# Widening a four-column constants tile to 128 columns in a fused retention and two-layer kernel

## The chip, the cores and the metric

The kernel runs on one core of one Trainium2 chip. The metric is the device time of one execution in microseconds; the kernel before takes 929.96 us, the median of three runs that lie between 928.1 and 932.1 us.

## The reference

The reference is a retention stage (attention with a decaying mask and no softmax) over 4 batches, 8 heads, 576 positions and head size 64, whose output is read as x with 2304 tokens and 512 features. Two layers follow, both 512 to 2048 to 512:

```
ret = (scale * q @ k.T) * Dmat            # Dmat[i, j] = gamma_h ** (i - j) for j <= i, else 0
x = (ret @ v), heads side by side         # 2304 x 512
h = x @ w_in;  g = max(0.01 * h, h);  x = g @ w_out       # layer 1
h = x @ w2_in; g = h - tanh(h);       out = g @ w2_out    # layer 2
```

## The kernel before, in words

**Precision.** Every matmul of the two layers works on a pair of fp32r tiles: a number is held as a rounded high part and the remainder (`xh` and `xl`; index 0 and 1 of `wp` and of `g`). A product is three matmuls: high by high, high by low, low by high. On the tensor engine each matmul has a stationary operand of 128 by 128, which a weight load brings in, and a moving operand of 128 by 512 or 128 by 256.

**Steps.** A layer goes over four groups of four blocks of 128 hidden features, and in each group over blocks of 512 tokens and one of 256. One step is one block of tokens with one block of features. Layer 1 has 60 steps of 512 tokens and 12 of 256 behind the retention stage, which itself carries the first 12 steps (256 tokens each) between its own matmuls. Layer 2 has 64 steps of 512 and 16 of 256. For each step the order of emission is the order on the engines:

- `h_mm` (L181): 12 matmuls, x moving (`xh`, `xl`, `xh` for each of four slices of features), the weights `wp` stationary.
- `act_a` and `chain`: ScalarE, VectorE and GpSimd make g from h. In layer 1 this is L193, L215, L224, L225; in layer 2 it is L201 to L207, L218 to L222, L224, L225. GpSimd has two operations for each step of layer 2: the product v (L203) and the low part of g (L225).
- `o_mm` (L251), two steps later: in layer 1 g moves and `wp` is stationary, in layer 2 `wp` moves and g is stationary. 12 matmuls in a step of 512 tokens.
- `evac` adds the result to `acc` at each fourth step.

While a group runs, the weights of the next are loaded as 64-bit numbers into `st`, narrowed on VectorE into `cw` and split into `wp` (L161 on ScalarE, L162 on GpSimd).

**Where the tiles lie.** Tiles are laid out along each partition in the order in which their pools are opened, each start rounded up to 32 bytes. The pool `keep` holds `xh`, `xl` and `acc` (36,864 bytes each, which is 72 times 512) and then `qb`, a tile of four fp32 constants. After it come the weight ring (`wp`, eight tiles of 4,096 bytes), the staging tiles (`st`), and then the pools of the stage: those of the retention first, and in their place those of the layers (`a`, `u`, `v`, `t`, `q`, `mk`, `g`, `cw`), all of which have sizes in multiples of 512 bytes. Before, `xh` begins at byte 16,512 and `qb` at byte 127,104, both 128 more than a multiple of 512. `qb` takes 16 bytes, so that the weight ring begins at byte 127,136, which is 160 more than a multiple of 512. The remainders by 512 are then 128 for `xh`, `xl` and `acc`; 160 for `wp`, `st` and for `g`, `cw` and the temporaries of the layers; 64 for the retention's `qk`, `kv`, `pt`, `st0`, `st1`, its `g` and its `cw`. Slices of x, `wp` and `g` that a matmul reads begin at multiples of 512 bytes from the start of the tile.

Of the kernel before, what the change touches and what calls it, by code (L numbers as in the profile page):

```python
# [10 lines left out]
F32 = mybir.dt.float32  # L11
# [7 lines left out]
P = 128  # L19
# [14 lines left out]
def retention_moe_moe(  # L34
# [28 lines left out]
    keep = ctx.enter_context(tc.tile_pool(name="keep", bufs=1))  # L63
# [5 lines left out]
    acc = keep.tile([P, KK * NT], F32, name="acc")  # L69
    acc_t = acc.rearrange("p (d t) -> p d t", d=KK)  # L70
    acc_n = acc.rearrange("p (t e) -> p t e", e=DM)
    qb = keep.tile([P, 4], F32, name="qb")

# [614 lines left out]
```

## Time and profile before

| what | value |
|---|---|
| median of three runs | 929.96 us |
| the profiled execution: its own time | 927.96 us |
| the profiled execution: span from first to last instruction | 926.1 us |
| outside the span | 1.9 us |
| mean granted TensorE clock, as a share of full speed | 0.992 |
| stretch of the retention stage | 0 to 143 us |
| stretch of layer 1 behind it | 143 to 512 us |
| stretch of layer 2 | 512 to 926 us |

Busy time is the time in which an engine has at least one instruction in work. Matmuls are pipelined: one takes longer than the distance from its start to the start of the next, so for the pace of TensorE the starts are read, and not the durations. PE is TensorE's matmul, PEld its weight load, DVE is VectorE, ACT is ScalarE, POOL is GpSimd.

### The profile page before, as it was taken

To read this page: it belongs to the slowest core of one execution; us is meant where nothing else is said; L and a number is where in the kernel's file an instruction comes from. 1 tells how busy PE (TensorE), PEld (TensorE's weight loads), DVE (VectorE), ACT (ScalarE), POOL (GpSimd) and SP (SyncE) were. 2 spreads that over 40 slices of the span, in tenths; PEclk is the share of its full clock that TensorE was granted. 3 is DMA by queue.
4 is the path that set the end of the run, shared out by engine and by line. 5 is a ranking of instruction groups with operands and counts; after the bars stand their busy time and mean duration, and the time that the engine had idled before them with its cause. 6 is when DMAs were issued, how large, how long until landed. Compare 5 with 4: busy or idle time off the path is not lost.

```text
span 926.1 us, 12850 instructions
## 1 busy us (share of the span) xinstructions
PE 886.5 (96%) x4832; PEld 739.7 (80%) x4832; DVE 597.6 (65%) x988; ACT 388.0 (42%) x777; POOL 468.5 (51%) x364
## 2 busy tenths in 40 slices
PE   5777999999999999999999999999999999999998
PEld 5677888888888888888888787888888877888886
DVE  5887656656573655546762677758785877755544
ACT  2343332233222322233334555675456455575554
POOL 3544422245223523354646855586557645595444
PEclk9989999999999999999999999999999999999999
DMA  7654421211110011101110011101110011001111
GB/s 276 212 174 150 155 99 47 91 46 46 46 63 30 24 46 69 45 1 46 46 69 24 23 46 69 47 0 46 47 69 24 23 46 69 1 1 46 45 46 69
DMA packets 21662, 58.36 MB, mean 63 GB/s; under 512 B 2528, under 2 KB 2912, under 8 KB 21600
## 3 DMA queue, kind: packets, MB, share of 16 engines
q1 hardware_dynamic: 21024, 57.16, 17.9%
q8 instruction: 38, 0.62, 0.3%
q10 hardware_dynamic: 576, 0.38, 0.1%
q14 instruction: 24, 0.20, 0.1%
HBM read 52.81 MB, written 4.72 MB: 62 GB/s over the span
## 4 chain that ended last, share of the span: by engine, by line
PE 60%; DVE 17%; POOL 11%; issue 6%; ACT 5%; DMA 1%; DVEq 0%; POOLq 0%; ACTq 0%
PE a L251 29%; PE h L181 28%; POOL v L203 5%; POOL g L225 4%; DVE v L219 4%; DVE v L222 3%; ACT g L224 2%; DVE acc L276 2%; DVE st L430 2%; DVE pt L396 2%; PE o L459 2%; POOL wp L162 1%; DVE cw L139 1%; ACT xh L468 1%; DVE cw L134 1%
## 5 line engine op out<-in xcount | busy, mean ns | idle before, releaser
L181 PE MATMUL h<-xh,wp 128*128 128x512 f32 (+1 forms) x1216 | 377.0, 375 | 0.0
L181 PEld LDWEIGHTS h<-xh,wp 128*128 128x128 f32 x1216 | 223.2, 188 | 45.2
L181 PE MATMUL h<-xl,wp 128*128 128x512 f32 (+1 forms) x608 | 228.3, 375 | 0.0
L251 PE MATMUL a<-wp,g 128*128 128x512 f32 x864 | 213.4, 393 | 5.2 <-POOL g L225 5.0
L251 PE MATMUL a<-g,wp 128*128 128x512 f32 (+1 forms) x1008 | 216.3, 364 | 1.9 <-POOL g L225 1.9
L225 POOL TENSOR_TENSOR g<-a,g 128x512 fp32r<-128x512 f32 (+1 forms) x84 | 107.7, 1283 | 197.8 <-ACT g L224 197.8
L251 PEld LDWEIGHTS a<-g,wp 128*128 128x128 f32 x1008 | 173.6, 192 | 32.3 <-POOL g L225 2.1
L251 PEld LDWEIGHTS a<-wp,g 128*128 128x128 f32 x864 | 160.9, 188 | 43.8 <-POOL g L225 9.2
L225 POOL TENSOR_TENSOR g<-v,g 128x512 fp32r<-128x512 f32 (+1 forms) x80 | 104.0, 1299 | 142.2 <-ACT g L224 142.2
L181 PEld LDWEIGHTS h<-xl,wp 128*128 128x128 f32 x608 | 114.7, 189 | 22.2
L162 POOL TENSOR_TENSOR wp<-cw,wp 128x512 fp32r<-128x512 f32 x64 | 90.4, 1421 | 55.1 <-ACT wp L161 54.6
L145 DVE SCALAR_TENSOR_TENSOR cw<-st,cw 128x512 uint32<-128x512 uint32 x128 | 116.1, 907 | 3.0
L224 ACT ACTIVATE g<-v 128x512 fp32r<-128x512 f32 (+1 forms) x80 | 47.2, 590 | 163.6 <-DVE v L222 162.5
L193 ACT ACTIVATE a<-h 128x512 f32<-128x512 f32 (+1 forms) x72 | 40.4, 562 | 172.0 <-PE h L181 172.0
L215 DVE TENSOR_TENSOR a<-h,a 128x512 f32<-128x512 f32 (+1 forms) x72 | 46.3, 643 | 101.0 <-ACT a L193 101.0
L203 POOL TENSOR_TENSOR v<-t,u 128x512 f32<-128x512 f32 (+1 forms) x80 | 101.9, 1273 | 11.9 <-ACT t L202 11.8
L276 DVE TENSOR_TENSOR acc<-a,acc 128x512 f32<-128x512 f32 (+1 forms) x114 | 72.0, 659 | 51.9 <-PE a L251 51.8
L219 DVE SCALAR_TENSOR_TENSOR v<-q,v 128x512 f32<-128x512 f32 (+1 forms) x80 | 58.3, 728 | 59.0 <-POOL v L203 58.0
L218 DVE TENSOR_TENSOR h<-h,t 128x512 f32<-128x512 f32 (+1 forms) x80 | 51.2, 640 | 48.4 <-ACT t L202 48.4
L224 ACT ACTIVATE g<-a 128x512 fp32r<-128x512 f32 (+1 forms) x84 | 47.9, 570 | 80.7 <-DVE a L215 80.7
L139 DVE TENSOR_SCALAR cw<-cw 128x512 uint32<-128x512 uint32 x64 | 63.4, 991 | 1.5
L222 DVE COPY_PREDICATED v<-mk,h 128x512 f32<-128x512 uint32 (+1 forms) x80 | 55.1, 688 | 8.2
(56 smaller groups left out, 745.9 us busy)
## 6 DMA issues: line engine op xcount, KB each, us to landing
st<-in_w1i SPq DMA_DIRECT2D x16, 512.0 KB, 3.3
st<-in_w1o SPq DMA_DIRECT2D x16, 512.0 KB, 3.3
st<-in_w2i SPq DMA_DIRECT2D x16, 512.0 KB, 3.2
st<-in_w2o SPq DMA_DIRECT2D x16, 512.0 KB, 3.2
kv<-in_vn SPq DMA_DIRECT2D x16, 320.0 KB, 4.3
qk<-in_qT SPq DMA_DIRECT2D x16, 288.0 KB, 2.9
qk<-in_kT SPq DMA_DIRECT2D x16, 288.0 KB, 3.4
out<-acc SPq DMA_DIRECT2D x18, 256.0 KB, 2.1
```

The lines of the kernel that those rows point to most:

```text
L139: nc.vector.tensor_scalar(out=t["w"], in0=t["w"], scalar1=3, scalar2=0x3FFFFFF8, op0=ALU.logical_shift_left, op1=ALU.bitwise_and,)
L145: nc.vector.scalar_tensor_tensor(out=t["w"], in0=t[src], scalar=scalar, in1=t["w"], op0=op, op1=ALU.bitwise_or)
L162: nc.gpsimd.tensor_tensor(out=wp[:, 1, :], in0=wf, in1=wp[:, 0, :].bitcast(F32), op=ALU.subtract)
L181: nc.tensor.matmul(out=ps[:, :n], lhsT=w[:, wi, cs], rhs=x[:, kk, t0:t0 + n], start=kk == 0 and i == 0, stop=kk == KK - 1 and i == 2,)
L203: nc.gpsimd.tensor_tensor(out=v[:, :n], in0=t_[:, :n], in1=u[:, :n], op=ALU.mult)
L218: nc.vector.tensor_tensor(out=h, in0=h, in1=t_, op=ALU.subtract)
L219: nc.vector.scalar_tensor_tensor(out=v, in0=q, scalar=RHO_A, in1=v, op0=ALU.add, op1=ALU.mult)
L222: nc.vector.copy_predicated(out=v, mask=mk.bitcast(U32), data=h)
L224: nc.scalar.activation(out=gt[:, 0, :n], in_=v, func=AF.Copy)
L225: nc.gpsimd.tensor_tensor(out=gt[:, 1, :n], in0=v, in1=gt[:, 0, :n].bitcast(F32), op=ALU.subtract)
L251: nc.tensor.matmul(out=o, lhsT=l, rhs=r, start=f == 0 and i == 0 and d % pack == 0, stop=f == GF - 1 and i == 2 and (d + 1) % pack == 0, s ...
L276: nc.vector.tensor_tensor(out=dst, in0=a, in1=dst, op=ALU.add)
```

## The change

The tile `qb` gets 128 columns in place of four, and so 512 bytes in place of 16 on each partition. Its four columns are written and read as before; the other 124 are never touched. No instruction is added, removed or moved.

```
     acc_n = acc.rearrange("p (t e) -> p t e", e=DM)
-    qb = keep.tile([P, 4], F32, name="qb")
+
+    qb = keep.tile([P, P], F32, name="qb")
```

Every tile behind `qb` moves up by 480 bytes: the weight ring begins at byte 127,616. The remainders by 512 become 128 for `wp`, `st`, `g`, `cw` and the temporaries of the layers, the same as that of x, and 32 for the retention's `qk`, `kv`, `pt`, `st0`, `st1`, `g` and `cw`. Those of `xh`, `xl` and `acc` stay at 128. The line numbers behind the edit grow by one.

## Rows read from the trace of the kernel before

**Rows 1.** Windows: length, PE, PEld, DVE, ACT, POOL busy us (instructions), clock, DMA share, GB/s.

```profile
0.00:143.00 143.00, 114.27 (x1277) 104.28 (x1278) 97.93 (x264) 46.48 (x140) 62.38 (x56) 0.96 0.52 173
143.00:512.00 369.00, 367.10 (x1725) 304.97 (x1724) 213.66 (x298) 110.22 (x197) 154.77 (x116) 1.00 0.13 46
512.00:926.00 414.00, 405.13 (x1834) 330.50 (x1833) 285.99 (x427) 231.27 (x441) 251.34 (x192) 1.00 0.11 40
```

**Rows 2.** Chain that ended last, by line: layer 1, then layer 2.

```profile
by line: PE h L181 48.1%; PE a L251 45.2%; POOL xl L281 1.7%; POOL g L225 1.3%; issue 1.3%; POOL wp L162 1.2%; DVE acc L276 0.9%; ACT xh L280 0.3%; ACT wp L161 0.1%; POOLq L162 0.0%; POOLq L225 0.0%
by line: PE a L251 20.8%; PE h L181 20.0%; POOL v L203 11.6%; DVE v L219 8.0%; POOL g L225 8.0%; issue 7.4%; DVE v L222 7.1%; ACT g L224 4.8%; DVE acc L276 3.3%; POOL wp L162 1.9%; DVE cw L139 1.3%; DVE h L218 1.0%; DVE cw L134 1.0%; DVE cw
```

**Rows 3.** Groups by form: shapes xcount | busy us, mean ns of one | idle before.

```profile
L181 PE MATMUL h<-xh,wp 128*128 128x512 f32 x992 | 332.8, 397 | 0.0
L251 PE MATMUL a<-wp,g 128*128 128x512 f32 x864 | 213.4, 393 | 5.2 <-POOL g L225 5.0
L181 PE MATMUL h<-xl,wp 128*128 128x512 f32 x496 | 196.7, 397 | 0.0
L251 PE MATMUL a<-g,wp 128*128 128x512 f32 x720 | 174.4, 391 | 0.0
...
L225 POOL TENSOR_TENSOR g<-a,g 128x512 fp32r<-128x512 f32 x60 | 86.7, 1445 | 144.4 <-ACT g L224 144.4
...
L281 POOL TENSOR_TENSOR xl<-acc,xh 128x512 fp32r<-128x512 f32 x16 | 22.7, 1449 | 12.7 <-ACT xh L280 12.7
```

**Rows 4.** Timeline of TensorE in layer 1: start us, us, instruction xcount.

```profile
396.49 2.91 PE L251 MATMUL a<-g,wp 128*128 128x512 f32 x12
399.24 0.40 PE L181 MATMUL h<-xh,wp 128*128 128x512 f32 x1
...
402.04 2.91 PE L251 MATMUL a<-g,wp 128*128 128x512 f32 x12
```

**Rows 5.** Timeline of TensorE from 397.9 to 398.9 us: late matmuls of one o_mm.

```profile
397.65 1.52 PE L251 MATMUL a<-g,wp 128*128 128x512 f32 x6
```

**Rows 6.** Timeline around 400.2 us: a matmul and the weight load beside it.

```profile
400.17 0.40 PE L181 MATMUL h<-xl,wp 128*128 128x512 f32 x1
400.17 0.19 PEld L181 LDWEIGHTS h<-xh,wp 128*128 128x128 f32 x1
```

**Rows 7.** Timeline of TensorE in layer 2.

```profile
599.36 1.52 PE L251 MATMUL a<-wp,g 128*128 128x512 f32 x6
600.72 0.40 PE L181 MATMUL h<-xh,wp 128*128 128x512 f32 x1
...
603.52 0.39 PE L251 MATMUL a<-wp,g 128*128 128x512 f32 x1
```

**Rows 8.** Timeline of TensorE, steps of 256 tokens in layer 1.

```profile
260.13 0.28 PE L181 MATMUL h<-xh,wp 128*128 128x256 f32 x1
...
261.55 1.60 PE L251 MATMUL a<-g,wp 128*128 128x256 f32 x12
262.99 0.40 PE L181 MATMUL h<-xh,wp 128*128 128x512 f32 x1
```

**Rows 9.** Timeline of TensorE at half clock, and the window with its clock.

```profile
466.06 0.63 PE L181 MATMUL h<-xh,wp 128*128 128x512 f32 x1
466.49 0.63 PE L181 MATMUL h<-xl,wp 128*128 128x512 f32 x1
...
466.06:467.50 1.44, 1.44 (x5) 1.15 (x5) 1.41 (x2) 0.00 (x0) 1.10 (x1) 0.50 0.00 0
```

**Rows 10.** Waits from 143 us on: us in total, times, longest.

```profile
POOL v L203 <- ACT t L202: 11.8, 10, 2.5
...
PE a L251 <- POOL g L225: 6.9, 9, 1.9
```

**Rows 11.** DMA issues: count, KB each, median us to landing.

```profile
st<-in_w1i SPq DMA_DIRECT2D x16, 512.0 KB, 3.3
...
qk<-in_qT SPq DMA_DIRECT2D x16, 288.0 KB, 2.9
```

## The prediction, made before the changed kernel was run

> **What bounds the kernel now.** I read the stages first. Behind the retention, TensorE is busy in 367.1 of 369 us of layer 1 and in 405.1 of 414 us of layer 2; in the retention it is busy in 114 of 143 us [rows 1]. The chain of waits says the same of layer 1, of which 93% is on TensorE's two lines, but not of layer 2, where TensorE holds 41% and the rest goes round GpSimd, VectorE and ScalarE [rows 2]. So layer 1 is as long as its matmuls, layer 2 is nearly so with a second loop close behind, and the retention is bound by other things.
>
> Since the change moves addresses alone, the next question is whether a matmul's pace depends on anything but its shape. In the timeline it does. Twelve matmuls of h_mm with 512 columns take 402.04 - 399.24 = 2.80 us, or 233.3 ns each; the twelve of the o_mm before them take 399.24 - 396.49 = 2.75 us, or 229.2 ns [rows 4]. The o_mm isn't even in itself. Its row seen from 397.9 us on begins at 397.65 us, so the first five take 397.65 - 396.49 = 1.16 us (232 ns each), and the others follow at (1.52 - 0.39) / 5 = 226 ns, or, up to the next h_mm, at (399.24 - 397.65) / 7 = 227 ns [rows 4, 5]. I take 226.7 ns for this settled pace. Layer 2, where the weights move and g stands still, shows the same: settled matmuls of o_mm at (1.52 - 0.39) / 5 = 226 ns, and 603.52 - 600.72 = 2.80 us for the h_mm [rows 7].
>
> At half the clock the difference is gone: two starts of h_mm are 0.43 us apart at a granted clock of 0.50, which is 512 columns at 1.2 GHz and nothing more [rows 9]. At 2.4 GHz the columns alone would take half of 426.7, 213.3 ns; so 13 ns in settled o_mm and 20 ns in h_mm are added by something that doesn't scale with the array. A weight load starts in the same instant as the matmul before which it is prefetched, and runs beside it [rows 6]: two streams read SBUF at once, the moving operand of one matmul and the stationary one of the next.
>
> The two kinds of call differ in the place of these streams. In o_mm both operands begin at 160 by 512, in either role; in h_mm the moving one begins at 128 and the stationary one at 160. My reading is that the two streams get in each other's way, that with equal remainders they fall into a rhythm with little loss, and with 32 bytes between them they never do. The five slow matmuls at the head of each o_mm are the time in which it settles after an h_mm.
>
> **The change part by part.** *h_mm with 512 columns.* x stays at 128, the weights go from 160 to 128, so the two become equal, as in o_mm. There are 992 + 496 = 1488 such matmuls [rows 3], 720 in layer 1 (60 steps by 12) and 768 in layer 2 (64 by 12). At 233.3 - 226.7 = 6.6 ns each that is 4.8 and 5.1 us of TensorE. Bounds: nothing, if the remainder isn't the cause; 233.3 - 213.3 = 20 ns, if equal remainders on a multiple of 64 remove all that is added.
>
> *o_mm with 512 columns.* Both of its operands go from 160 to 128 together. With no change of rhythm between the calls, its first five matmuls should be like its last seven: 2.75 - 12 * 0.2267 = 0.03 us per call, which the rounding of the rows leaves at 0.02 to 0.03; I take 0.025. 1584 matmuls [rows 3] make 132 calls' worth, 60 in layer 1 and 72 in layer 2: 1.5 and 1.8 us. Bounds: a loss of 233.3 - 229.2 = 4.1 ns each, if h_mm is slow because its moving operand starts at a multiple of 64, and a gain of 229.2 - 213.3 = 15.9 ns.
>
> *Steps of 256 columns.* Here settling costs something. An h_mm takes 261.55 - 260.13 = 1.42 us, and an o_mm at equal remainders 262.99 - 261.55 = 1.44 us [rows 8]. If h_mm goes over to the second figure, 12 such steps in layer 1 lose 0.2 us and 16 in layer 2 lose 0.3 us. Those within the retention lie beside other waits (TensorE is idle for 29 us there) and cost nothing; without that cover 12 steps by 0.02 us would be 0.24 us.
>
> *What else moves.* GpSimd's subtraction takes 1449 ns where all three operands lie at 128, and 1445 ns where they lie at 160 [rows 3], so I put the other engines' new addresses at nothing, with 4 ns either way as the bound. Staging tiles that lie at 160, 32 more than a multiple of 64, take 512 KB in 3.3 us, the retention's tiles at 64 take 288 KB in 2.9 us [rows 11]; so a start that is no multiple of 64 isn't dearer by the byte, and the retention's loads, which now get one, are put at nothing. If they were dearer, they are issued two pairs ahead and DMA is busy in 52% of that stage [rows 1]. The retention's own matmuls have both operands moved by the same 480 bytes; nothing, with 1 us either way for a stage in which TensorE isn't the bound. `qb` itself is written and read in the same four columns.
>
> *What reaches the end.* Layer 1: 4.8 + 1.5 - 0.2 = 6.1 us, all of it, since the chain there is TensorE's. Layer 2: 5.1 + 1.8 - 0.3 = 6.6 us of TensorE, but the loop of v on GpSimd, two VectorE operations, ScalarE's g and GpSimd's g is nearly as long as a step. In the whole of layer 2 GpSimd waited for h (through ScalarE's tanh) only 11.8 us, and TensorE for g 6.9 us [rows 10]. So the loop alone would shorten this layer by at most 11.8 us, and what TensorE gains will partly turn up as more waits for g, above all where a new group's weights are split on GpSimd. Between none of the 6.6 us and all of it I take half, 3.3 us, because the two reserves are of like size. The sum is 6.1 + 3.3 = 9.4 us. The profiled execution took 927.96 us, so 918.6 us; it lay 2.0 us below the median of the runs, so 920.6 us as a median. With none or all of layer 2's share the same sum gives 923.9 and 917.3 us, and with the spread of the runs (about 2 us to each side) 915 to 926 us.
>
> **The rivals.** *The remainder isn't the cause.* h_mm differs from o_mm in other ways: its twelve matmuls add into one bank of PSUM, and x is moved from four slices far apart. Then nothing moves: 930 us. Against it: twelve into one bank against three into one should make o_mm uneven at every third matmul, and what is seen is five slow and seven even ones [rows 4, 5]. For it: no call in this trace has x's remainder and the weights' equal.
> The Trainium skill speaks for this rival, in "SBUF — State Buffer", section "Who interferes with whom": it gives TensorE two independent read ports, for the moving operand and for the weight load, and says that TensorE never waits on anyone. By it the time stays at 930 us; by the rows two calls of one shape differ by 4.1 ns per matmul, which the rule can't explain, so I don't follow it.
>
> *A moving operand that starts at a multiple of 64 is the slow one.* The rows can't part this from my reading, since in the layers whatever moves from 128 is x against weights at 160. Then h_mm stays at 233.3 ns, and o_mm, now from 128 too, goes from 229.2 to 233.3 ns: 1584 * 4.1 = 6.5 us more of TensorE, which passes whole, since TensorE is the bound: 936.5 us. It decides once both operands at 128 run slower than both at 160. Against it: a start on a boundary would have to be worse than one off it.
>
> *Equal and on a boundary is better still.* Both streams then begin at a multiple of 64, which no call does now. If nothing is added any more, layer 1 gains 720 * 20 + 720 * 15.9 = 25.8 us, and layer 2 at most the 11.8 us of its loop: 929.96 - 37.6 = 892 us. For it are only the half-clock rows, where nothing is added [rows 9].
> The Trainium skill, "TensorE: Matmul & The Clock Gate", section "Wait — 56ns, not 53.3ns?", gives about 2.5 ns above the columns for matmuls in a row at full clock, so 215.8 ns here; by that estimate this case would gain some 22 us in layer 1 in place of 25.8. No row here comes under 226 ns.
>
> **How the numbers follow.** The forecast has a chance of 0.68, no effect 0.17, the slow boundary 0.10, the better boundary 0.05. The time is the forecast's, 920.6 us, its own range 915 to 926. The range of 914 to 932 us takes in the case without effect with the spread of its runs and leaves out the last two cases, 0.15 together. About 0.5%, 4.6 us, is what a measurement can tell from no change: the forecast reaches that in all but 0.05 of its chance (when layer 2 gives nothing and the runs fall badly), so faster is 0.63 + 0.05 = 0.68, within 0.5% is 0.05 + 0.16 = 0.21, and slower is 0.10 + 0.01 = 0.11.
>
> **What would show it.** Right: in a timeline of layer 1 a call of h_mm takes 2.72 us and one of o_mm 2.72 us with no slow head; mean durations of the h matmuls fall from 397 to about 390 ns; layer 1 is some 6 us shorter and layer 2 some 3 us, with TensorE's wait for g above 6.9 us and GpSimd's wait for tanh below 11.8 us; h_mm of 256 columns takes 1.44 us. Wrong: h_mm still at 2.80 us (no effect), o_mm at 2.80 us (slow boundary), either at less than 2.70 us (better boundary), or a shorter pace of both calls with layer 2 as long as before, in which case the loop was the bound.

## The result, and the profile after

The changed kernel takes 921.06 us (median of ten runs, 917.69 to 924.71) against 929.88 us of the kernel before (median of ten runs too): a ratio of 0.9904, with a 95% interval of 0.9884 to 0.9923. The forecast was 920.6 us. The profiled execution took 920.59 us with a span of 918.8 us, 7.3 us less than before.

Where those 7.3 us come from is seen when both executions are cut at the first h_mm behind the retention and at the first h_mm of layer 2. The windows of the kernel after are these (length, then busy us and instructions of PE, PEld, DVE, ACT, POOL, the clock, DMA share and GB/s):

```profile
0.00:144.30 144.30, 116.20 (x1280) 105.95 (x1280) 100.09 (x266) 46.85 (x140) 62.46 (x56) 0.95 0.51 171
144.30:503.90 359.60, 357.75 (x1706) 301.68 (x1705) 213.02 (x296) 109.88 (x196) 152.02 (x114) 1.00 0.14 47
503.90:918.80 414.90, 403.38 (x1849) 332.83 (x1848) 285.46 (x427) 231.27 (x442) 253.91 (x195) 1.00 0.11 40
```

The same cuts in the kernel before:

```profile
0.00:143.40 143.40, 114.67 (x1280) 104.68 (x1280) 98.33 (x266) 46.48 (x140) 62.38 (x56) 0.96 0.52 172
143.40:508.60 365.20, 363.30 (x1707) 301.81 (x1706) 213.26 (x296) 109.85 (x196) 152.03 (x114) 1.00 0.13 47
508.60:926.10 417.50, 408.53 (x1849) 333.26 (x1847) 285.99 (x427) 231.65 (x441) 254.07 (x195) 1.00 0.11 40
```

Layer 1 is 5.6 us shorter and layer 2 is 2.6 us shorter; the retention was 0.9 us longer in this execution. In the two layers no other engine's busy time moved by more than 0.6 us, and that of TensorE's matmuls fell by 5.55 us in layer 1 and by 5.15 us in layer 2.

The timeline of TensorE in layer 1 answers to [rows 4]:

```profile
390.72 0.39 PE L182 MATMUL h<-xh,wp 128*128 128x512 f32 x1
...
393.44 2.88 PE L252 MATMUL a<-g,wp 128*128 128x512 f32 x12
396.16 0.39 PE L182 MATMUL h<-xh,wp 128*128 128x512 f32 x1
...
398.88 2.88 PE L252 MATMUL a<-g,wp 128*128 128x512 f32 x12
```

Both calls now take the same time: h_mm 393.44 - 390.72 = 2.72 us where it took 2.80, o_mm 396.16 - 393.44 = 2.72 us where it took 2.75. Layer 2 shows it too, against [rows 7]:

```profile
598.13 2.88 PE L252 MATMUL a<-wp,g 128*128 128x512 f32 x12
600.85 0.39 PE L182 MATMUL h<-xh,wp 128*128 128x512 f32 x1
...
603.57 2.66 PE L252 MATMUL a<-wp,g 128*128 128x512 f32 x11
```

The groups by form say it of all matmuls of 512 columns (busy us, mean ns of one, idle before); against [rows 3] the h matmuls fell from 397 to 390 ns:

```profile
L182 PE MATMUL h<-xh,wp 128*128 128x512 f32 x992 | 326.5, 390 | 0.0
...
L252 PE MATMUL a<-wp,g 128*128 128x512 f32 x864 | 213.2, 392 | 7.8 <-POOL g L226 7.5
L182 PE MATMUL h<-xl,wp 128*128 128x512 f32 x496 | 193.6, 390 | 0.0
L252 PE MATMUL a<-g,wp 128*128 128x512 f32 x720 | 173.1, 389 | 0.0
```

In steps of 256 columns (timeline of layer 1, against [rows 8]) h_mm went from 1.42 to 257.59 - 256.16 = 1.43 us, and o_mm stayed at 259.03 - 257.59 = 1.44 us:

```profile
256.16 0.28 PE L182 MATMUL h<-xh,wp 128*128 128x256 f32 x1
...
257.59 1.60 PE L252 MATMUL a<-g,wp 128*128 128x256 f32 x12
259.03 0.28 PE L182 MATMUL h<-xh,wp 128*128 128x256 f32 x1
```

The waits from the end of the retention on (us in total, times, longest) show why layer 2 gained less than TensorE did. Against [rows 10], TensorE's matmuls wait 9.3 us for g in place of 6.9, and GpSimd 9.5 us for the tanh in place of 11.8. The weight loads of o_mm, which in layer 2 bring in g, wait 15.5 us in place of 11.3. So the loop has come nearer to being the bound. The weight loads' line of the kernel before, and then the lines of the kernel after:

```profile
PEld a L251 <- POOL g L225: 11.3, 12, 2.1
```

```profile
PEld a L252 <- POOL g L226: 15.5, 17, 2.1
POOL v L204 <- ACT t L203: 9.5, 8, 2.4
PE a L252 <- POOL g L226: 9.3, 13, 1.9
```

### The profile page after: what moved, and what is told of

Its sections match the earlier page's. It is cut to its first block, busy times and chain, and to the rows that moved or that the text cites. A ratio compares the mean times of both kernels' runs of the same rounds, so it can differ in the third digit from the quotient of the medians.

```text
span 918.8 us, 12850 instructions
## 1 busy us (share of the span) xinstructions
PE 877.3 (95%) x4832; PEld 740.5 (81%) x4832; DVE 598.6 (65%) x988; ACT 388.0 (42%) x777; POOL 468.4 (51%) x364
## 4 chain that ended last, share of the span: by engine, by line
PE 62%; DVE 16%; POOL 10%; issue 6%; ACT 4%; DMA 1%; ACTq 0%; DVEq 0%; POOLq 0%
PE a L252 30%; PE h L182 29%; POOL v L204 4%; POOL g L226 3%; DVE v L220 3%; DVE v L223 3%; DVE acc L277 2%; ACT g L225 2%; DVE st L431 2%; PE o L460 2%; DVE pt L397 2%; DVE cw L140 1%; POOL wp L163 1%; DVE cw L135 1%; ACT xh L469 1%
## 5 line engine op out<-in xcount | busy, mean ns | idle before, releaser
L182 PE MATMUL h<-xh,wp 128*128 128x512 f32 (+1 forms) x1216 | 371.1, 371 | 0.0
L182 PE MATMUL h<-xl,wp 128*128 128x512 f32 (+1 forms) x608 | 225.3, 371 | 0.0
L252 PE MATMUL a<-g,wp 128*128 128x512 f32 (+1 forms) x1008 | 213.8, 361 | 1.9 <-POOL g L226 1.9
```

The lines of the kernel that those rows point to most:

```text
L182: nc.tensor.matmul(out=ps[:, :n], lhsT=w[:, wi, cs], rhs=x[:, kk, t0:t0 + n], start=kk == 0 and i == 0, stop=kk == KK - 1 and i == 2,)
L252: nc.tensor.matmul(out=o, lhsT=l, rhs=r, start=f == 0 and i == 0 and d % pack == 0, stop=f == GF - 1 and i == 2 and (d + 1) % pack == 0, s ...
```

## The experiments

The theory going in: a matmul is slower when its operands' two streams begin at unequal places, and equal remainders let them run with less loss. The rivals: what counts is a multiple of 64; only the distance by 64 counts; h_mm is slow for reasons of its own. And for layer 2: a loop over GpSimd takes part of the gain. The edits are against the kernel before unless the text says otherwise.

| kernel | x, wp, g by 512 | h_mm, o_mm in layer 1 | layers 1 and 2 | median | ratio to before (95%) |
|---|---|---|---|---|---|
| before | 128, 160, 160 | 2.80, 2.75 us | 365.2, 417.5 us | 929.88 | |
| changed | 128, 128, 128 | 2.72, 2.72 us | 359.6, 414.9 us | 921.06 | 0.9904 (0.9884 to 0.9923) |
| equal_160 | 160, 160, 160 | 2.73, 2.71 us | 359.6, 414.8 us | 918.54 | 0.9895 (0.9868 to 0.9922) |
| apart_64 | 128, 192, 192 | 2.80, 2.74 us | 364.7, 417.1 us | 927.94 | 0.9991 (0.9971 to 1.0010) |
| apart_128 | 128, 256, 256 | 2.79, 2.74 us | 362.9, 417.1 us | 927.23 | 0.9976 (0.9957 to 0.9996) |
| apart_256 | 128, 384, 384 | 2.72, 2.72 us | 359.6, 414.7 us | 923.17 | 0.9943 (0.9924 to 0.9962) |
| g_apart | 128, 128, 160 | 2.76, 2.80 us | 365.7, 417.2 us | 928.87 | 0.9989 (0.9972 to 1.0007) |

Each ratio is against the kernel before as it ran beside that kernel, and the columns of lengths are from the profiled execution of each, cut as above; the calls are differences of starts in the timelines.

One thing more is in the lengths of layer 1. Between 457 and 468 us TensorE stands idle once, for just under 2 us, waiting for g. Behind that wait its granted clock is 0.50, 1.2 GHz, for some microseconds in most of the profiles, but not in those of apart_128 and of the two lightened kernels below. The windows from 457 to 472 us show it (clock 0.89 and 1.00), of apart_64 and then of apart_128:

```profile
457.00:472.00 15.00, 13.05 (x79) 11.81 (x78) 11.52 (x16) 4.38 (x10) 8.75 (x8) 0.89 0.22 70
```

```profile
457.00:472.00 15.00, 13.16 (x86) 11.89 (x85) 11.96 (x16) 4.81 (x10) 9.96 (x8) 1.00 0.22 70
```

Layer 1, whose code is the same in the lightened kernels, took 363.6 us in light_before and 358.1 us in light_after, without that stretch, against 365.2 and 359.6 us with it; so it is worth some 1.5 us, and most of what apart_128 seems to gain in layer 1 is this.

**equal_160: equal, but no multiple of 64.** A tile of 32 bytes goes ahead of x, and `qb` is widened.

```
+    pad = keep.tile([P, 8], F32, name="pad")
     xh = keep.tile([P, KK, NT], F32R, name="xh")
...
-    qb = keep.tile([P, 4], F32, name="qb")
+    qb = keep.tile([P, P], F32, name="qb")
```

> x, the weights and g all begin at 160 by 512, equal but no multiple of 64. If the equal remainder is what counts: about 921 us, a call of h_mm and one of o_mm both 2.72 us in the timeline. If the multiple of 64 is what counts: about 930 us, h_mm at 2.80 us. If only the distance by 64 counts: about 921 us.

Measured: 918.54 us, and the timeline of layer 1 below: h_mm takes 394.92 - 392.19 = 2.73 us, o_mm 397.63 - 394.92 = 2.71 us.

```profile
392.19 0.39 PE L182 MATMUL h<-xh,wp 128*128 128x512 f32 x1
...
394.92 2.88 PE L252 MATMUL a<-g,wp 128*128 128x512 f32 x12
397.63 0.39 PE L182 MATMUL h<-xh,wp 128*128 128x512 f32 x1
```

A multiple of 64 isn't needed; with it falls the rival of the slow boundary, in either direction, since starts on and off it give the same layers within 0.1 us.

**apart_64, apart_128 and apart_256: multiples of 64, unequal.** `qb` gets 16, 32 and 64 columns.

```
-    qb = keep.tile([P, 4], F32, name="qb")
+    qb = keep.tile([P, 16], F32, name="qb")    # apart_64; 32 and 64 columns in the others
```

> x at 128, the weights and g at 192 by 512: both multiples of 64, 64 bytes apart. If the equal remainder by 512 counts: about 930 us, h_mm at 2.80 us. If a multiple of 64 counts, or the distance by 64: about 921 us, h_mm at 2.72 us.

> x at 128, the weights and g at 256 by 512: multiples of 64, 128 bytes apart. If the equal remainder by 512 counts: about 930 us, h_mm at 2.80 us. If a multiple of 64 counts, or the distance by 64: about 921 us, h_mm at 2.72 us.

> x at 128, the weights and g at 384 by 512: multiples of 64, 256 bytes apart. If the equal remainder by 512 counts: about 930 us, h_mm at 2.80 us. If a multiple of 64 counts, or the distance by 64: about 921 us, h_mm at 2.72 us. If the rhythm repeats every 256 bytes: about 921 us here alone of the three distances.

Measured: at 64 and 128 bytes apart h_mm is slow as before, 396.14 - 393.34 = 2.80 us and 396.60 - 393.81 = 2.79 us; at 256 bytes apart it is fast, 393.37 - 390.65 = 2.72 us for the o_mm and 396.09 - 393.37 = 2.72 us for the h_mm. The timelines of layer 1 of apart_64, apart_128 and apart_256, in this order:

```profile
390.60 2.90 PE L251 MATMUL a<-g,wp 128*128 128x512 f32 x12
393.34 0.39 PE L181 MATMUL h<-xh,wp 128*128 128x512 f32 x1
...
396.14 2.90 PE L251 MATMUL a<-g,wp 128*128 128x512 f32 x12
```

```profile
391.07 2.90 PE L251 MATMUL a<-g,wp 128*128 128x512 f32 x12
393.81 0.40 PE L181 MATMUL h<-xh,wp 128*128 128x512 f32 x1
...
396.60 2.90 PE L251 MATMUL a<-g,wp 128*128 128x512 f32 x12
```

```profile
390.65 2.88 PE L251 MATMUL a<-g,wp 128*128 128x512 f32 x12
393.37 0.39 PE L181 MATMUL h<-xh,wp 128*128 128x512 f32 x1
...
396.09 2.88 PE L251 MATMUL a<-g,wp 128*128 128x512 f32 x12
```

So both theories of 64 fall, and mine is corrected: the remainders by 512 needn't be equal. At 32, 64 and 128 bytes apart the matmuls of h_mm are slow; at 0 and 256 they are fast, which is what equal remainders by 256 would give. No other distance was run. The two layers of apart_256 are those of the changed kernel (359.6 and 414.7 us); its median is 2.1 us above, and its profiled execution spent 147.0 us in the retention, of which more below.

**g_apart: the other call is made the slow one.** Against the changed kernel, 32 bytes ahead of the layers' g. `cw`, which lies behind g and which no matmul reads, moves with it; x and `wp` stay.

```
+            pd = mc.enter_context(tc.tile_pool(name="pd", bufs=1))
+            pd.tile([P, 8], F32, name="pad")
             pools["g"] = mc.enter_context(tc.tile_pool(name="g1", bufs=3))
```

> The changed kernel with 32 bytes ahead of the layers' g alone: x and the weights stay equal at 128, g goes to 160. If the distance by 256 between the two operands of a matmul decides: h_mm stays at 2.72 us but for a head in which it settles, o_mm goes to 2.80 us in both layers, in layer 1 with g moving and in layer 2 with g stationary, and the time to about 928 us. If x or h_mm is special and o_mm is fast anywhere: about 921 us.

Measured: 928.87 us, as slow as the kernel before. In layer 1 (g moving) and layer 2 (g stationary) o_mm now takes 396.32 - 393.52 and 647.70 - 644.90, 2.80 us both, and h_mm, whose own operands are equal, 2.76 us in layer 1 and 2.73 us in layer 2. The timelines of layer 1, and then of layer 2:

```profile
393.52 2.97 PE L252 MATMUL a<-g,wp 128*128 128x512 f32 x12
396.32 0.40 PE L182 MATMUL h<-xh,wp 128*128 128x512 f32 x1
...
399.08 2.97 PE L252 MATMUL a<-g,wp 128*128 128x512 f32 x12
```

```profile
642.17 0.39 PE L182 MATMUL h<-xh,wp 128*128 128x512 f32 x1
...
644.90 2.96 PE L252 MATMUL a<-wp,g 128*128 128x512 f32 x12
647.70 0.39 PE L182 MATMUL h<-xh,wp 128*128 128x512 f32 x1
```

Nothing is special about x, the four slices or the one bank of PSUM: the slowness goes where the unequal pair goes, in either role, and the other call, with its equal pair, pays a little for settling.

**light_before and light_after: layer 2 without GpSimd's product.** In both kernels, v is no longer made on GpSimd, and VectorE takes u in its place, so that g lacks the factor tanh in this product.

```
-        nc.gpsimd.tensor_tensor(out=v[:, :n], in0=t_[:, :n], in1=u[:, :n], op=ALU.mult)
...
-                out=v, in0=q, scalar=RHO_A, in1=v, op0=ALU.add, op1=ALU.mult
+                out=v, in0=q, scalar=RHO_A, in1=u, op0=ALU.add, op1=ALU.mult
```

> The kernel before without GpSimd's product in layer 2, so that layer 2's g lacks a factor and GpSimd has one operation a step in place of two. If the loop over GpSimd holds layer 2 back beside TensorE: layer 2 loses the waits of TensorE for g, about 7 us, and takes some 410 us; if TensorE alone sets it: no change, 417 us.

> The changed kernel with the same product left out. If the loop took what layer 2 did not gain: layer 2 is shorter than in the lightened kernel before by TensorE's whole gain, 6 to 7 us, in place of 2.7 us. If something else took it: by 2.7 us again.

Measured: 924.6 us (ratio 0.9935, 0.9911 to 0.9959) and 910.61 us (0.9783, 0.9763 to 0.9804). The windows of layer 2, light_before and then light_after:

```profile
510.70:921.80 411.10, 405.99 (x1849) 333.40 (x1847) 278.77 (x427) 236.39 (x441) 150.90 (x115) 1.00 0.12 40
```

```profile
503.80:908.60 404.80, 399.41 (x1849) 333.49 (x1847) 278.34 (x427) 235.80 (x441) 151.04 (x115) 1.00 0.12 41
```

With the loop shortened, the alignment gives 411.1 - 404.8 = 6.3 us in layer 2, where it gave 2.6 us with the loop in place, and TensorE's busy time falls by 405.99 - 399.41 = 6.6 us. The rest of the gain had gone into waits for g: the weight loads' waits, which grew by 4.2 us between the full kernels, are alike here (light_before, then light_after).

```profile
PEld a L250 <- POOL g L224: 4.2, 3, 2.1
```

```profile
PEld a L251 <- POOL g L225: 4.4, 3, 2.1
```

**v_on_vector and v_in_chain: the loop shortened with nothing left out.** Against the changed kernel, the product is computed on VectorE: first where it stood, among the operations of act_a, then one step later at the head of the chain. In both, the line on GpSimd goes.

```
-        nc.gpsimd.tensor_tensor(out=v[:, :n], in0=t_[:, :n], in1=u[:, :n], op=ALU.mult)
+        nc.vector.tensor_tensor(out=v[:, :n], in0=t_[:, :n], in1=u[:, :n], op=ALU.mult)   # v_on_vector
...
             v, t_, q, mk, u = (x[:, :n] for x in tmp.pop(s))
+            nc.vector.tensor_tensor(out=v, in0=t_, in1=u, op=ALU.mult)                    # v_in_chain
```

> The changed kernel with layer 2's product of tanh and the square on VectorE in place of GpSimd, nothing left out. If the loop over GpSimd is what holds layer 2 back: layer 2 falls from 414.9 us towards the 404.9 us of the lightened kernel, and the time to between 911 and 917 us, since the product takes 0.7 us on VectorE where it took 1.3 us. If VectorE, which then has some 340 us of work in this layer beside its narrowing of weights, becomes the bound around the change of groups: 921 us or more.

> The same product on VectorE, but emitted at the head of the chain a step later, when its inputs have long been made, so that nothing behind it on VectorE waits for ScalarE. If the 129 us of VectorE's waits for the tanh made the kernel with the product on VectorE slow, and the loop over GpSimd limits layer 2 otherwise: layer 2 falls below 414.9 us, to 405 to 411 us, and the time to 911 to 917 us. If VectorE's work itself is too much: 921 us or more.

Measured: the first is a miss, 975.17 us (ratio 1.0493, 1.0457 to 1.0528), with layer 2 at 467.7 us. VectorE isn't too busy there (313 us of 468); it stands still, since everything behind the product on its queue waits with it for the tanh (waits of v_on_vector):

```profile
DVE v L204 <- ACT t L203: 129.5, 76, 2.7
...
PE a L252 <- POOL g L226: 24.0, 42, 1.9
```

The second takes 916.15 us (914.77 to 919.95; ratio 0.9862, 0.9826 to 0.9899), the shortest of the kernels that leave nothing out, though its interval overlaps that of the change alone. In its profile layer 2 takes 410.1 us, 4.8 us less than in the changed kernel, although TensorE's granted clock fell in it (0.84 from 525 to 536 us) and in the changed kernel's layer 2 did not:

```profile
508.00:918.10 410.10, 401.99 (x1849) 334.67 (x1847) 327.51 (x507) 231.66 (x441) 155.93 (x115) 1.00 0.12 40
```

**after_again: the retention stage once more.** The changed kernel, unaltered.

> The changed kernel once more, unaltered. If the retention stage is really 0.9 us longer with its tiles at 32 in place of 64: 144 us again up to the first matmul of layer 1 behind it. If that was the spread of one execution: another length, between 143 and 147 us.

Measured: one execution of 919.53 us, with 143.4 us up to layer 1, as in the kernel before:

```profile
0.00:143.40 143.40, 114.11 (x1281) 104.27 (x1281) 97.24 (x266) 46.80 (x140) 62.29 (x56) 0.93 0.53 172
143.40:503.00 359.60, 357.75 (x1707) 301.67 (x1706) 212.99 (x296) 109.89 (x196) 152.04 (x114) 1.00 0.15 47
```

So the new addresses aren't needed to explain the 0.9 us: the same kernel took 144.3 and 143.4 us. Over the profiled executions of all these kernels that stage took from 143.4 to 148.4 us, while layer 1 of the changed kernel took 359.6 us in both of its profiles; of the 1.1 us between these two, 0.9 us lie in the retention. The mean granted clock of that stage differed too, from 0.90 to 0.96 over the first 143 us; what this costs was not tested. Whether the place of the retention's tiles adds to the spread stays open: equal_160, whose retention tiles lie at 64 as in the kernel before, took 145.8 us.

## Why the prediction was right, point by point

- *Two streams, one rhythm.* The reading of the two calls as one shape with two placements was right, and the experiments bear it out in both directions: equal_160 makes h_mm fast, g_apart makes o_mm slow. What is shown is that the distance between the starts of a matmul's operands sets its pace at full clock, at the five distances that were run. That the weight load beside the matmul is what it collides with was argued from [rows 6] and [rows 9] and not tested: no run took the weight load away. That the difference is gone at half clock rested on unequal operands alone [rows 9]; the changed kernel's h_mm, with equal ones, supplies the other side, (462.28 - 461.43) / 2 = 0.43 us from start to start at a granted clock of 0.50 (timeline, and the window with its clock):

```profile
461.43 0.63 PE L182 MATMUL h<-xh,wp 128*128 128x512 f32 x1
...
462.28 1.05 PE L182 MATMUL h<-xh,wp 128*128 128x512 f32 x2
...
461.43:463.56 2.13, 2.13 (x7) 1.65 (x6) 2.06 (x4) 0.42 (x1) 1.12 (x1) 0.50 0.21 85
```

- *h_mm, 6.6 ns for each matmul.* Measured (2.80 - 2.72) / 12 = 6.7 ns.
- *o_mm, 0.025 us for each call by losing its slow head.* Measured 0.03 us in layer 1 by the starts, and (174.4 - 173.1) / 60 = 0.02 us by the busy time of its group. In layer 2 the mean fell only from 393 to 392 ns, with waits for g in between. The forecast took layer 2 for 72 calls; it has 80, since each of the 16 steps of 256 tokens has a call of six matmuls and a head of its own, which would have added 0.2 us.
- *Steps of 256 columns, 0.02 us lost for each.* Measured 0.01 us.
- *Layer 1, 6.1 us.* Measured 5.6 us. Of the half microsecond 0.2 us are o_mm's, 1.3 us in place of 1.5; the rest was not followed up.
- *Layer 2, half of 6.6 us.* TensorE's 6.6 us were right, as the lightened pair shows; the share that comes through was 2.6 us, two fifths, and the mechanism was the one named, the loop over GpSimd. The half itself was a choice between none and all, so that it came near is in part luck.
- *The retention, nothing.* Right as far as the spread of its length lets one tell.
- *The sum.* 9.4 us forecast, 8.8 us measured between the medians (929.88 and 921.06). In the profiled executions the two layers gave 5.6 + 2.6 = 8.2 us of it; the rest of the 8.8 us no run assigns to a stage.
- *The rivals.* No effect, at 930 us, is out. The slow boundary is out by the changed kernel, whose o_mm with both operands at 128 takes 2.72 us and not 2.80, and by equal_160. The better boundary didn't come either: with every start on a multiple of 64 a matmul still takes 2.72 / 12 = 226.7 ns. The Trainium skill, "SBUF — State Buffer", section "Who interferes with whom", holds that TensorE's two read ports are independent and that TensorE never waits on anyone. What the prediction drew from it, no change of the time, did not come: in g_apart 32 bytes ahead of g took o_mm from 2.72 to 2.80 us. Whether it is these two ports that meet, no run here shows. The Trainium skill, "TensorE: Matmul & The Clock Gate", section "Wait — 56ns, not 53.3ns?", gives about 2.5 ns above the columns at full clock, which makes 215.8 ns an estimate here. No run reaches it: the fast calls take 2.71 to 2.73 us for twelve matmuls.

## What to carry to other kernels

Compare the pace of calls that have the same shape, from the starts in the timeline: a difference that the schedule doesn't explain can be a matter of where the operands lie, and a tile of a few bytes ahead of large ones can put them apart. Where matmuls set the time, let the moving and the stationary operands begin at the same remainder by 256 bytes, and check it after every tile that is added ahead of them. Before a gain on the busiest engine is counted in full, look how close the next loop is. Its waits, 11.8 us here, are no measure of what comes through: of TensorE's 6.6 us the layer kept 2.6 while 9.5 us of those waits were left, and 6.3 us once the loop was shortened.

## What the runs showed of the hardware that was not expected

- The pace goes with the distance by 256 bytes, as far as it was run: operands 0 or 256 bytes apart give 226.7 ns for 512 columns of fp32r with a weight load beside it, and 32, 64 or 128 bytes give about 233 ns (2.79 to 2.80 us for twelve); whether the starts are multiples of 64 makes no difference (2.72 us for twelve with all at 128, 2.71 to 2.73 us with all at 160).
- It is no plain gain: at 256 columns equal remainders take 1.43 to 1.44 us for twelve, against 1.42 us at 32 bytes apart. The distances don't rank there as they do at 512 columns, since h_mm at 128 bytes apart takes 259.01 - 257.58 = 1.43 us too (apart_128):

```profile
257.58 0.28 PE L181 MATMUL h<-xh,wp 128*128 128x256 f32 x1
...
259.01 1.60 PE L251 MATMUL a<-g,wp 128*128 128x256 f32 x12
```

- A call with an equal pair behind one with an unequal pair needs some matmuls to settle: h_mm in g_apart took 2.76 us in layer 1 and 2.73 us in layer 2 in place of 2.72, as o_mm had taken 2.75 in the kernel before.
